# First-layer weight pieces split by one cast and one subtraction, and an expert's sums copied out one step earlier

## The chip, the cores and the metric

The kernel runs on one core of a Trainium2 chip. The metric is the device time of one execution in microseconds; the time quoted for a kernel is the median of several runs. The engines that matter here are TensorE (PE, matrix products; PEld is its weight load), VectorE (DVE), ScalarE (ACT), GpSimd (POOL) and SyncE (SP), whose queue issues nearly all DMAs. Each engine works through its own instructions in order, and the engines wait for one another by semaphores.

## The reference

Three layers follow one another. A recurrence over 768 positions for 4 x 8 heads gives 3072 tokens of width 320. Each token then goes to one of 8 experts (a two-layer network with ReLU), and the result goes through a dense two-layer network with a leaky ReLU:

```
x = attn_out.transpose(0, 2, 1, 3).reshape(3072, 320)
...
h = np.maximum(np.einsum('ecd,edf->ecf', disp, w1), 0.0)     # w1: 8 x 320 x 1024
y = np.einsum('ecf,efd->ecd', h, w2)                         # w2: 8 x 1024 x 320
out[i] = gate_w[i] * y[expert_idx[i], pos[i]]
...
h = x @ w_in                                                 # 320 x 2048
out = np.maximum(0.01 * h, h) @ w_out                        # 2048 x 320
```

## The kernel before

The recurrence fills the first 537 us of the profiled execution, the experts 537 to 810 us, the dense network the rest. The change touches the second and third of these, in the function `moe`.

**Split numbers.** Products are made in a rounded 32-bit format. So that nothing is lost, each operand is split in two: the rounded value (a cast, on ACT) and the rest (a subtraction on DVE). A first-layer weight matrix has 320 rows, 128 + 128 + 64. A piece `q` of it covers all 320 rows and 512 columns; it is loaded into one of two buffers `raw` of 128 x 1536, the last 64 rows into partitions 0 to 63 of the third part (L946, L947). `split(n)` makes the tile `wq` of it, six parts of 512 columns: for the 256 full rows by one cast (L961) and one subtraction (L964); for the 64 last rows by a cast for part 5 (L962), a cast to the other half of the partitions for part 4 (L963), a subtraction (L965), and a cast of that rest back into part 5 (L966), so that parts 5 and 4 hold in 128 partitions what their two products need. A piece `o` (second-layer weights, L972 to L975) has no such remainder.

**Steps.** An expert has eight blocks m = 0 to 7 of 128 hidden units. Step i of the loop makes in this order: `do_a(i)`, the eight first-layer products of block i into `ph` (L1000), then ReLU into `gh` on ACT (L1051) and the rest `gl` on DVE (L1052); on m = 0, 2, 4, 6 `split` of a piece that is needed an expert later (q, q, o, o) and the load of the piece after next; a part of a repacking of 64-bit weights, in 22 portions, that POOL and DVE share (`cv1`: POOL L1102 to L1104; `cv2`: DVE L1113 to L1116, then POOL L1117; `cv0` loads a portion, `cv3` writes one back, L1122); on m = 2, 4, 6 the transposes of the next expert's tokens (L1035 to L1041); and last `do_b(i-2)`, the eight second-layer products of the block two steps back, added up in the PSUM tiles y0, y1, y2 (L1065 to L1068). After the last block of an expert `do_b` copies the sums out: y0 on ACT (L1071), y1 on DVE (L1072), y2 on both (L1073, L1074). There is one buffer for each of y0, y1, y2, so the next expert's first second-layer products wait for these copies.

Below, *boundary k* (k = 1 to 7) is the place where PE turns from expert k-1's sums to expert k's. At step i = 8k+1 the copies of expert k-1 are issued; at step 8k+2 come the first products of expert k into y0.

**The first layer's product** of one block is eight matmuls: for each of the two full parts rounded x rounded, rounded x rest, rest x rounded (L996), and two for the 64 last rows (L998), where `xt` part 4 holds the rounded tokens in its lower half and their rest in its upper half.

Of the kernel before, what the change touches and what calls it, by code (L numbers as in the profile page):

```python
# [10 lines left out]
ALU = mybir.AluOpType  # L11
# [914 lines left out]
def moe(ctx, tc, I, out, R, eng, wi):  # L926

    nc = tc.nc
    V, A, P, T, S = eng
# [10 lines left out]
    def load(n):  # L940
        if n >= len(pieces):
            return
        kind, i = pieces[n]
        r = raws[n] = R.raws[n % 2]
        if kind == 'q':
            S.dma_start(r[:, 0:1024], I['wqa'][i] if i < 16 else wi[0][i - 16])  # L946
            S.dma_start(r[0:64, 1024:1536], I['wqb'][i] if i < 16 else wi[1][32 * (i - 16):32 * (i - 16) + 32].rearrange("p (r f) -> (p r) f", f=512))  # L947
        else:
            S.dma_start(r[:, 0:1280], I['wo'][i] if i < 16 else wi[2][i - 16])

    def split(n):
        if n >= len(pieces):
            return
        kind, i = pieces[n]
        r = raws.pop(n)
        if kind == 'q':
            t = kp.tile([128, 6, 512], F32R, tag="wq", name="wq", bufs=4)
            wqs[i] = t
            tf = t.bitcast(F32)
            r3 = r.rearrange("p (c f) -> p c f", c=3)  # L960
            A.copy(t[:, 0:2], r3[:, 0:2])  # L961
            A.copy(t[0:64, 5], r3[0:64, 2])  # L962
            A.copy(t[64:128, 4], r3[0:64, 2])  # L963
            V.tensor_tensor(t[:, 2:4], r3[:, 0:2], tf[:, 0:2], ALU.subtract)  # L964
            V.tensor_tensor(t[0:64, 4], r3[0:64, 2], tf[0:64, 5], ALU.subtract)  # L965
            A.copy(t[64:128, 5], tf[0:64, 4])  # L966
        else:
            t = kp.tile([128, 4, 640], F32R, tag="wo", name="wo", bufs=4)
            wos[i] = t
            tf = t.bitcast(F32)  # L970
            r3 = r[:, 0:1280].rearrange("p (k c) -> p k c", k=4)
            A.copy(t[:, :, 0:320], r3)  # L972
            if i < 16:
                V.tensor_tensor(t[:, :, 384:640], r3[:, :, 0:256], tf[:, :, 0:256], ALU.subtract)
                V.tensor_tensor(t[:, :, 320:384], r3[:, :, 256:320], tf[:, :, 256:320], ALU.subtract)  # L975
            else:
                V.tensor_tensor(t[:, :, 320:640], r3, tf[:, :, 0:320], ALU.subtract)
# [14 lines left out]
    def gemm_a(ph, n, xt, wq, mm):  # L992
        o = 128 * mm
        seq = []
        for c in range(2):
            seq += [(wq[:, c, o:o + 128], xt[:, c, 0:n]), (wq[:, c, o:o + 128], xt[:, 2 + c, 0:n]), (wq[:, 2 + c, o:o + 128], xt[:, c, 0:n])]  # L996

        seq += [(wq[:, 5, o:o + 128], xt[:, 4, 0:n]), (wq[:, 4, o:o + 128], xt[:, 4, 0:n])]  # L998
        for k, (l, r) in enumerate(seq):
            T.matmul(ph, l, r, start=k == 0, stop=k == 7)  # L1000

# [2 lines left out]
    def prep_g(g):  # L1004
        if g < NG:
            o, n = GRP[g]
            sl = slice(o, o + n)
            split_x(('g', g), n, [Y[:, 0, sl], Y[:, 1, sl]], Y[0:64, 2, sl])
            S.dma_start(gid[:, g, 0:n // 128], R.ctab[sl].rearrange("(b p) c -> p b c", p=128))


    with ExitStack() as c1:
# [3 lines left out]
        def load_x(e):  # L1016
            if e >= NE:
                return
            w = cx.tile([TW, 4, XC], F32, tag="win", name="win", bufs=2)
            wins[e] = w  # L1020
            R.after(S.dma_start(w, R.xs[e * REG:e * REG + WIN].rearrange("(k p) c -> p k c", p=TW)), R.puts)
# [23 lines left out]
        def do_a(i):  # L1045
            e, m = divmod(i, 8)
            ph = ps.tile([128, 512], F32, tag="h", name="ph", bufs=3)[:, 0:WIN]
            gemm_a(ph, WIN, xts[e], wqs[2 * e + m // 4], m % 4)
            gh = kp.tile([128, 512], F32R, tag="gh", name="gh", bufs=3)
            gl = kp.tile([128, 512], F32R, tag="gl", name="gl", bufs=3)  # L1050
            A.activation(gh[:, 0:WIN], ph, AF.Relu)  # L1051
            V.scalar_tensor_tensor(gl[:, 0:WIN], ph, 0.0, gh.bitcast(F32)[:, 0:WIN], ALU.max, ALU.subtract)  # L1052
            gs[i] = gh, gl

        def do_b(i):
            e, m = divmod(i, 8)
            if m == 0:
                ys[e] = [ps.tile([128, 512], F32, tag=f"y{c}", name=f"y{c}", bufs=1)[:, 0:WIN] for c in range(3)]
            y = ys[e]
            gh, gl = gs.pop(i)  # L1060
            gh, gl = gh[:, 0:WIN], gl[:, 0:WIN]
            wo = wos[2 * e + m // 4][:, m % 4]
            for c in range(3):
                hi = wo[:, 128 * c:128 * c + 128]
                T.matmul(y[c], hi, gh, start=m == 0, stop=False)  # L1065
                if c < 2:
                    T.matmul(y[c], wo[:, 384 + 128 * c:512 + 128 * c], gh, start=False, stop=False)
                T.matmul(y[c], hi, gl, start=False, stop=m == 7)  # L1068
            if m == 7:
                at = ds(R.base[e], WIN)  # L1070
                A.copy(Y[:, 0, at], y[0])  # L1071
                V.tensor_copy(Y[:, 1, at], y[1])  # L1072
                A.copy(Y[0:64, 2, at], y[2][64:128])  # L1073
                V.tensor_tensor(Y[0:64, 2, at], y[2][0:64], Y[0:64, 2, at], ALU.add)  # L1074
                R.after(S.dma_start(R.ctab[at], R.xs[e * REG:e * REG + WIN, D:D + 2]), R.puts)
# [15 lines left out]
        def cv0(k):  # L1091
            if 0 <= k < len(cv):
                cs[k] = cx.tile([128, 1024], I32, tag="cv", name="cv", bufs=2)
                S.dma_start(cs[k][:, 0:2 * cv[k][2]], cv[k][0].bitcast(I32))

        def cv1(k):
            if 0 <= k < len(cv):
                n = cv[k][2]
                hl = cs[k][:, 0:2 * n].rearrange("p (c two) -> p c two", two=2)
                h = hl[:, :, 1].bitcast(F32)  # L1100
                m = cx.tile([128, 512], F32, tag="cvm", name="cvm", bufs=2)[:, 0:n]
                P.tensor_tensor(m, h, h, ALU.mult)  # L1102
                P.tensor_scalar(m, m, THR * THR, None, ALU.is_ge)  # L1103
                P.tensor_tensor(m, m, h, ALU.mult)  # L1104
                cs[k] = hl, m

        def cv2(k):
            if 0 <= k < len(cv):
                n = cv[k][2]
                hl, m = cs.pop(k)  # L1110
                lo, a = hl[:, :, 0].bitcast(mybir.dt.uint32), hl[:, :, 1]
                g = cx.tile([128, 512], I32, tag="cvg", name="cvg", bufs=1)[:, 0:n]
                V.tensor_scalar(a, m.bitcast(I32), 0x07FFFFFF, 3, ALU.bitwise_and, ALU.logical_shift_left)  # L1113
                V.scalar_tensor_tensor(g, m.bitcast(I32), -0x40000000, a, ALU.bitwise_and, ALU.bitwise_or)
                V.tensor_scalar(a, g, -0x00800000, None, ALU.bitwise_and)
                V.scalar_tensor_tensor(m, lo, 2.0 ** -52, a.bitcast(F32), ALU.mult, ALU.mult)  # L1116
                P.tensor_tensor(m, m, g.bitcast(F32), ALU.add)  # L1117
                cs[k] = m

        def cv3(k):  # L1120
            if 0 <= k < len(cv):
                S.dma_start(cv[k][1], cs.pop(k))  # L1122
# [9 lines left out]
        load(4); load(5)  # L1132
        kc = 0
        for i in range(8 * NE + 2):
            if i < 8 * NE:
                e, m = divmod(i, 8)
                do_a(i)
                at = (0, 2, 4, 6) if e else (2, 3, 5, 6)
                if m in at:
                    n = 4 * (e + 1) + at.index(m)  # L1140
                    split(n)
                    load(n + 2)
                if i == 3:
                    R.places()
                if m == 5:
                    R.place(e)
                if m == 4:
                    load_x(e + 2)
                if i == 2:
                    cv0(0)  # L1150
                    cv0(1)
                elif i == 4:
                    cv1(0)
                elif i > 4 and m in (3, 5, 7):
                    cv3(kc - 1)
                    cv2(kc)
                    cv0(kc + 2)
                elif i > 4 and m in (0, 4, 6):
                    cv1(kc + 1)
                    kc += 1  # L1160
                if m in (2, 4, 6):
                    prep_x1(e + 1, (m - 2) // 2)
            if i >= 2:
                do_b(i - 2)
            if i == 8 * NE - 2:
                prep_g(0)
# [276 lines left out]
```

## Time and profile before

| | us |
|---|---|
| median of 3 runs (1154.49, 1155.58, 1165.28) | 1155.58 |
| the profiled execution | 1167.16 |
| its span, first to last instruction | 1165.4 |
| PE busy | 987.0 (85%) |
| DVE busy | 796.7 (68%) |
| ACT busy | 630.8 (54%) |
| POOL busy | 479.8 (41%) |
| mean granted TensorE clock | 0.922 |

Busy shares are averages over stages that differ: PE is busy 75% of the time in the first 537 us and 98% in the last 340. The granted clock is given as a share of full speed: 1.00 is 2.4 GHz and 0.50 is 1.2 GHz, and values between are means over a stretch in which both occur. In a timeline a row is one instruction, or several alike, with its start, its length, and in brackets the idle time of its engine just before it and what ended that. A recorded length of a DVE or POOL instruction can hold time in which it stood still after its start.

### The profile page before, as it was taken

To read this page: it belongs to the slowest core of one execution; us is meant where nothing else is said; L and a number is where in the kernel's file an instruction comes from. 1 tells how busy PE (TensorE), PEld (TensorE's weight loads), DVE (VectorE), ACT (ScalarE), POOL (GpSimd) and SP (SyncE) were. 2 spreads that over 40 slices of the span, in tenths; PEclk is the share of its full clock that TensorE was granted. 3 is DMA by queue.
4 is the path that set the end of the run, shared out by engine and by line. 5 is a ranking of instruction groups with operands and counts; after the bars stand their busy time and mean duration, and the time that the engine had idled before them with its cause. 6 is when DMAs were issued, how large, how long until landed. Compare 5 with 4: busy or idle time off the path is not lost.

```text
span 1165.4 us, 32129 instructions
## 1 busy us (share of the span) xinstructions
PE 987.0 (85%) x13099; PEld 874.8 (75%) x13099; DVE 796.7 (68%) x1877; ACT 630.8 (54%) x1486; POOL 479.8 (41%) x575
## 2 busy tenths in 40 slices
PE   4566777977777878995998888989999999999997
PEld 3455666766666667774887777878989999999997
DVE  8986878999999969434776667776664545343453
ACT  6144577867777688994544444444543434343343
POOL 7334336545556446201354435452639191000100
PEclk9766799979989889997998889999999999999999
DMA  7539465455554532423654455643201010000000
GB/s 207 191 80 258 125 184 149 134 121 135 152 114 125 145 81 56 115 54 109 217 170 143 150 164 155 183 138 112 93 22 57 15 44 6 18 12 12 23 13 14
DMA packets 132459, 125.19 MB, mean 107 GB/s; under 512 B 90448, under 2 KB 98256, under 8 KB 132304
## 3 DMA queue, kind: packets, MB, share of 16 engines
q1 hardware_dynamic: 130000, 115.17, 35.3%
q0 software_dynamic: 2304, 7.89, 1.9%
q8 instruction: 105, 1.72, 0.6%
q14 instruction: 50, 0.41, 0.1%
HBM read 98.86 MB, written 24.20 MB: 106 GB/s over the span
## 4 chain that ended last, share of the span: by engine, by line
PE 38%; DVE 16%; ACT 12%; issue 10%; POOL 5%; DMA 4%; SPq 1%; POOLq 0%; ACTq 0%; DVEq 0%
PE ph L1000 14%; PE py L641 4%; ACT Z L294 3%; PE oy L1204 3%; PE oy L1203 3%; PE oy L1202 3%; ACT NI L294 2%; DVE Tt L472 2%; DVE tmp L470 2%; DMA wc<-cvm 2%; ACT MV L294 1%; POOL cvm L1103 1%; PE tr L609 1%; PE y L1065 1%; PE ch L589 1%
## 5 line engine op out<-in xcount | busy, mean ns | idle before, releaser
L1000 PE MATMUL ph<-xt,wq 128*128 128x512 f32 (+2 forms) x1408 | 318.4, 370 | 1.9 <-DVE xt L1041 1.9
L1000 PEld LDWEIGHTS ph<-xt,wq 128*128 128x128 f32 x1408 | 254.4, 194 | 33.0 <-DVE xt L1041 2.7
L1182 DVE TENSOR_TENSOR gf<-gf,ph 128x512 f32<-128x512 f32 (+1 forms) x112 | 68.4, 611 | 102.3 <-ACT gf L1181 102.0
L1186 DVE TENSOR_TENSOR gl<-gf,gh 128x512 fp32r<-128x512 f32 (+1 forms) x112 | 76.0, 679 | 70.1 <-ACT gh L1185 70.1
L294 ACT COPY Z<-tr 40x512 f32<-40x512 f32 x192 | 101.0, 539 | 39.6 <-PE tr L609 36.9
L1181 ACT ACTIVATE gf<-ph 128x512 f32<-128x512 f32 (+1 forms) x112 | 60.0, 535 | 110.0 <-PE ph L1000 109.7
L1212 POOL DMA_INDIRECT out_dram<-ob,gid x24 | 23.9, 996 | 221.9 <-ACT ob L1211 216.7
L1185 ACT CAST gh<-gf 128x512 fp32r<-128x512 f32 (+1 forms) x112 | 62.6, 559 | 91.9 <-DVE gf L1182 91.9
L641 PE MATMUL py<-Z,RE 128*32 128x40 f32 x1536 | 78.8, 215 | 24.2 <-DVE RE L630 24.0
L1065 PE MATMUL y<-gh,wo 128*128 128x448 f32 x192 | 76.1, 397 | 22.5 <-ACT Y L1071 22.5
L641 PEld LDWEIGHTS py<-Z,RE 128*32 128x32 f32 x1536 | 68.9, 122 | 32.0 <-DVE RE L630 27.1
L1204 PE MATMUL oy<-wo,gl 128*128 128x320 f32 x288 | 89.2, 310 | 0.2 <-DVE gl L1186 0.2
L1202 PE MATMUL oy<-wo,gh 128*128 128x320 f32 x288 | 88.9, 309 | 0.0
L1203 PE MATMUL oy<-wo,gh 128*128 128x320 f32 x288 | 88.9, 309 | 0.0
L1051 ACT ACTIVATE gh<-ph 128x448 fp32r<-128x448 f32 x64 | 34.8, 544 | 91.0 <-PE ph L1000 90.7
L472 DVE TENSOR_TENSOR Tt<-Tt,tmp 128x30 f32<-128x30 f32 (+19 forms) x275 | 77.0, 311 | 0.6
L1068 PE MATMUL y<-gl,wo 128*128 128x448 f32 x192 | 73.7, 384 | 0.0
L609 PE MATMUL tr<-ident,MV 128*104 128x128 f32 x384 | 63.4, 298 | 9.5 <-DVE AE L422 4.9
L470 DVE TENSOR_TENSOR tmp<-Mu,Tt 128x30 f32<-128x30 f32 (+19 forms) x275 | 68.1, 277 | 0.7
L1117 POOL TENSOR_TENSOR cvm<-cvm,cvg 128x512 f32<-128x512 f32 (+1 forms) x22 | 26.2, 1191 | 94.9 <-DVE cvm L1116 94.9
L630 DVE TENSOR_TENSOR RE<-tr,maskP 64x128 f32<-64x128 f32 x144 | 41.4, 287 | 34.7 <-PE tr L622 17.8
L589 PE MATMUL ch<-MV,NI 128*40 128x40 f32 x1472 | 53.8, 221 | 13.1 <-issue 6.2
(185 smaller groups left out, 2340.6 us busy)
## 6 DMA issues: line engine op xcount, KB each, us to landing
KB<-in_kbT_dram SPq DMA_DIRECT2D x24, 512.0 KB, 5.3
RE<-in_rT_dram SPq DMA_DIRECT2D x48, 256.0 KB, 3.6
AE<-in_aT_dram SPq DMA_DIRECT2D x20, 512.0 KB, 5.3
raw<-in_wo_dram SPq DMA_DIRECT2D x16, 640.0 KB, 4.2
raw<-in_wqa_dram SPq DMA_DIRECT2D x16, 512.0 KB, 4.5
w<-in_wT_dram SPq DMA_DIRECT2D x24, 264.0 KB, 4.5
xs<-maskZ SPq DMA_DIRECT2D x8, 563.5 KB, 9.2
win<-xs SPq DMA_DIRECT2D x8, 563.5 KB, 6.7
```

Source lines behind the costliest of these rows:

```text
L294: (E.copy if E is A else E.tensor_copy)(o, i)
L470: op(e, d, lambda E, tv=tv, k=k, lo=lo, h=h, m=m: E.tensor_tensor(tv, Mu[:, k:k + 1, k + 1:].broadcast_to([128, h - lo, m]), Tt[:, lo:h, k ...
L472: op(e, d, lambda E, tv=tv, k=k, lo=lo, h=h: E.tensor_tensor(Tt[:, lo:h, k + 1:], Tt[:, lo:h, k + 1:], tv, ALU.subtract), [('tmp', x)], [t ...
L609: E.transpose(c['t'][0:104, q, :], MV[:, 4 * h + q], ident)
L641: E.matmul(py[32 * g:32 * g + 32, b, col:col + 40], RE[:, j, p, :], Z[:, p, ZC[j]:ZC[j] + 40], start=True, stop=True)
L1000: T.matmul(ph, l, r, start=k == 0, stop=k == 7)
L1065: T.matmul(y[c], hi, gh, start=m == 0, stop=False)
L1068: T.matmul(y[c], hi, gl, start=False, stop=m == 7)
L1186: V.tensor_tensor(gl, gf, gh.bitcast(F32), ALU.subtract)
L1202: T.matmul(o, gh[:, sl], w[:, 0:320], start=m == 0, stop=False)
L1203: T.matmul(o, gh[:, sl], w[:, 320:640], start=False, stop=False)
L1204: T.matmul(o, gl[:, sl], w[:, 0:320], start=False, stop=m == 15)
```

## The change

Four edits. The 64 last rows are loaded twice, into both halves of the partitions. The split of a q piece becomes one cast and one subtraction over all 1536 columns; the six parts of `wq` are now three rounded ones and three rests. The products take them from their new places, with the same eight matmuls. And at step 8k+1 `do_b` of the last block of expert k-1, with the copies, is put ahead of `do_a` and everything else in that step.

```
-            S.dma_start(r[0:64, 1024:1536], I['wqb'][i] if i < 16 else ...)
+            for o in (0, 64):
+                S.dma_start(r[o:o + 64, 1024:1536], I['wqb'][i] if i < 16 else ...)
...
-            A.copy(t[:, 0:2], r3[:, 0:2])
-            A.copy(t[0:64, 5], r3[0:64, 2])
-            A.copy(t[64:128, 4], r3[0:64, 2])
-            V.tensor_tensor(t[:, 2:4], r3[:, 0:2], tf[:, 0:2], ALU.subtract)
-            V.tensor_tensor(t[0:64, 4], r3[0:64, 2], tf[0:64, 5], ALU.subtract)
-            A.copy(t[64:128, 5], tf[0:64, 4])
+            A.copy(t[:, 0:3], r3)
+            V.tensor_tensor(t[:, 3:6], r3, tf[:, 0:3], ALU.subtract)
...
-            seq += [..., (wq[:, 2 + c, o:o + 128], xt[:, c, 0:n])]
+            seq += [..., (wq[:, 3 + c, o:o + 128], xt[:, c, 0:n])]
-        seq += [(wq[:, 5, o:o + 128], xt[:, 4, 0:n]), (wq[:, 4, o:o + 128], xt[:, 4, 0:n])]
+        seq += [(wq[:, 2, o:o + 128], xt[:, 4, 0:n]), (wq[:, 5, o:o + 128], xt[:, 4, 0:n])]
...
         for i in range(8 * NE + 2):
+            last = i >= 2 and (i - 2) % 8 == 7
+            if last:
+                do_b(i - 2)
             if i < 8 * NE:
                 e, m = divmod(i, 8)
                 do_a(i)
...
-            if i >= 2:
+            if i >= 2 and not last:
                 do_b(i - 2)
```

In the changed program the lines behind the split stand three lower in number: the cast is L962 (ACT), the subtraction L963 (DVE), the doubled load L948, the first-layer products L997, the copies of the sums L1068 to L1071, the repacking's first DVE line L1110, its write-back L1119.

DVE at boundary 2, before: from the `gl` of expert 2's block 0 over the split of that step (m = 0) and the copies of expert 1's sums to the first row of the split at m = 2 (`Y` is the tile that takes the sums).

```order
L1052 SCALAR_TENSOR_TENSOR gl_9958<-ph_9948,gh_9957 128x448
L964 TENSOR_TENSOR wq_9961<-raw0_76,wq_9961 128x1024
L965 TENSOR_TENSOR wq_9961<-raw0_76,wq_9961 64x512
L1052 SCALAR_TENSOR_TENSOR gl_9991<-ph_9981,gh_9990 128x448
L1072 ISA
L1072 COPY Y_9357<-y1_9765 128x448
L1074 ISA
L1074 TENSOR_TENSOR Y_9357<-y2_9766,Y_9357 64x448
L1052 SCALAR_TENSOR_TENSOR gl_10017<-ph_10007,gh_10016 128x448
L964 TENSOR_TENSOR wq_10020<-raw1_77,wq_10020 128x1024
```

The same place in the changed program:

```order
L1049 SCALAR_TENSOR_TENSOR gl_9942<-ph_9932,gh_9941 128x448
L963 TENSOR_TENSOR wq_9945<-raw0_76,wq_9945 128x1536
L1069 ISA
L1069 COPY Y_9357<-y1_9747 128x448
L1071 ISA
L1071 TENSOR_TENSOR Y_9357<-y2_9748,Y_9357 64x448
L1049 SCALAR_TENSOR_TENSOR gl_9984<-ph_9974,gh_9983 128x448
L1049 SCALAR_TENSOR_TENSOR gl_9997<-ph_9987,gh_9996 128x448
L963 TENSOR_TENSOR wq_10000<-raw1_77,wq_10000 128x1536
```

The two subtractions are one, and the copies of y1 and y2 stand right behind it; the `gl` of the next block has moved behind them.

ACT at the same place, before: the split of the step m = 0, the next `gh`, and the copies of expert 1's sums.

```order
L961 CAST wq_9961<-raw0_76 128x1024
L962 CAST wq_9961<-raw0_76 64x512
L963 CAST wq_9961<-raw0_76 64x512
L966 CAST wq_9961<-wq_9961 64x512
L1051 ACTIVATE gh_9990<-ph_9981 128x448
L1071 ISA
L1071 COPY Y_9357<-y0_9764 128x448
L1073 ISA
L1073 COPY Y_9357<-y2_9766 64x448
```

And in the changed program:

```order
L962 CAST wq_9945<-raw0_76 128x1536
L1068 ISA
L1068 COPY Y_9357<-y0_9746 128x448
L1070 ISA
L1070 COPY Y_9357<-y2_9748 64x448
L1048 ACTIVATE gh_9983<-ph_9974 128x448
```

Four casts, the last of which took its input from DVE, are one that takes it from the load alone; the copies stand right behind it and ahead of the next `gh`.

SP's queue in the middle of expert 1, before: the loads of a q piece, the next expert's tokens (`win`), and the write-back of a repacked portion (`wb`).

```order
L946 DMA raw0_76<-in_wqa_dram 128x1024
L947 DMA raw0_76<-in_wqb_dram 64x512
L1021 DMA win_9824<-xs_60 112x4x322
L918 TENSOR_LOAD bi_75
L1122 DMA wb_81<-cvm_9697 128x512
```

And in the changed program:

```order
L946 DMA raw0_76<-in_wqa_dram 128x1024
L948 DMA raw0_76<-in_wqb_dram 64x512 x2
L1018 DMA win_9807<-xs_60 112x4x322
L918 TENSOR_LOAD bi_75
L1119 DMA wb_81<-cvm_9683 128x512
```

One more load of 128 KB stands ahead of the write-back. On PE the eight products of expert k-1's last block come ahead of the first-layer products of step 8k+1 instead of behind them; their number and sizes are the same.

## Rows read from the trace of the kernel before

**Rows 1.** Waits between 537 and 810 us: who for whom, total us, times, longest.

```profile
ACT wq L966 <- DVE wq L965: 47.1, 17, 7.2
DVE cv L1113 <- POOL cvm L1104: 28.5, 12, 4.9
...
PE y L1065 <- ACT Y L1071: 22.5, 7, 4.7
```

**Rows 2.** Stretches (length, PE, PEld, DVE, ACT, POOL busy, clock, DMA share, GB/s).

```profile
587.05:594.52 7.47, 4.98 (x18) 4.28 (x17) 4.82 (x7) 5.79 (x10) 3.36 (x3) 0.77 0.37 94
594.52:618.41 23.89, 23.89 (x125) 22.00 (x123) 17.87 (x26) 8.58 (x14) 12.55 (x10) 1.00 0.61 185
618.41:628.18 9.77, 5.88 (x18) 5.13 (x17) 6.99 (x9) 5.88 (x10) 4.90 (x3) 0.65 0.38 106
...
685.94:696.48 10.54, 5.84 (x19) 5.09 (x18) 7.77 (x10) 5.87 (x10) 4.51 (x4) 0.68 0.46 123
...
754.19:759.14 4.95, 3.68 (x19) 3.03 (x18) 3.71 (x6) 4.47 (x8) 2.36 (x2) 1.00 0.46 133
784.20:792.27 8.07, 5.22 (x18) 4.37 (x17) 5.34 (x7) 5.34 (x9) 3.89 (x3) 0.79 0.33 90
```

**Rows 3.** Timeline of PE around boundary 2.

```profile
609.91 1.78 PE L1000 MATMUL ph<-xt,wq 128*128 128x448 f32 x8
...
613.15 1.78 PE L1000 MATMUL ph<-xt,wq 128*128 128x448 f32 x8
...
618.01 0.55 PE L1035 MATMUL pt<-ident,win 112*128 112x112 f32 x4
622.45 0.74 PE L1065 MATMUL y<-gh,wo 128*128 128x448 f32 x1 [3.89 <-ACT Y L1071]
...
628.18 0.36 PE L1065 MATMUL y<-gh,wo 128*128 128x448 f32 x1
```

**Rows 4.** Timeline of ACT around boundary 2.

```profile
613.75 0.62 ACT L963 CAST wq<-raw 64x512 fp32r<-64x512 f32 x1
620.78 0.62 ACT L966 CAST wq<-wq 64x512 fp32r<-64x512 f32 x1 [6.41 <-DVE wq L965]
...
621.87 0.53 ACT L1071 COPY Y<-y 128x448 f32 x1
```

**Rows 5.** Timeline of DVE around boundary 2.

```profile
614.50 0.43 DVE L1113 TENSOR_SCALAR cv<-cvm 128x512 int32<-128x512 int32 x1 [3.60 <-POOL cvm L1104]
...
616.77 0.62 DVE L1052 SCALAR_TENSOR_TENSOR gl<-ph,gh 128x448 fp32r<-128x448 f32 x1
617.30 2.01 DVE L964 TENSOR_TENSOR wq<-raw,wq 128x1024 fp32r<-128x1024 f32 x1
619.23 1.52 DVE L965 TENSOR_TENSOR wq<-raw,wq 64x512 fp32r<-64x512 f32 x1
...
622.54 0.62 DVE L1072 COPY Y<-y 128x448 f32 x1
...
624.49 1.23 DVE L964 TENSOR_TENSOR wq<-raw,wq 128x1024 fp32r<-128x1024 f32 x1 [0.28 <-ACT wq L961]
625.63 0.68 DVE L965 TENSOR_TENSOR wq<-raw,wq 64x512 fp32r<-64x512 f32 x1
```

**Rows 6.** Timeline of POOL around boundary 2.

```profile
616.93 1.30 POOL L1117 TENSOR_TENSOR cvm<-cvm,cvg 128x512 f32<-128x512 f32 x1 [2.46 <-DVE cvm L1116]
618.18 2.02 POOL L1102 TENSOR_TENSOR cvm<-cv 128x512 f32<-128x512 f32 x1
```

**Rows 7.** Chain that ended last, from boundary 2 to 3 (start, us, what).

```profile
637.44 6.57 DMA wc<-cvm
...
648.12 0.44 DVE cv L1113
```

**Rows 8.** A stretch of the same columns as above, behind the loads.

```profile
641.50:644.00 2.50, 2.50 (x14) 2.31 (x14) 1.71 (x4) 0.55 (x1) 0.00 (x0) 1.00 1.02 345
```

**Rows 9.** DMA issues by line: times, KB each, median us to landing.

```profile
raw<-in_wqb_dram SPq DMA_DIRECT2D x16, 128.0 KB, 4.6
```

More of the change, by code (lines that the diff above doesn't have):

```diff
@@ L946, in load @@
             S.dma_start(r[:, 0:1024], I['wqa'][i] if i < 16 else wi[0][i - 16])
-            S.dma_start(r[0:64, 1024:1536], I['wqb'][i] if i < 16 else wi[1][32 * (i - 16):32 * (i - 16) + 32].rearrange("p (r f) -> (p r) f", f=512))
+            for o in (0, 64):
+                S.dma_start(r[o:o + 64, 1024:1536], I['wqb'][i] if i < 16 else wi[1][32 * (i - 16):32 * (i - 16) + 32].rearrange("p (r f) -> (p r) f", f=512))
         else:
@@ L995, in gemm_a @@
         for c in range(2):
-            seq += [(wq[:, c, o:o + 128], xt[:, c, 0:n]), (wq[:, c, o:o + 128], xt[:, 2 + c, 0:n]), (wq[:, 2 + c, o:o + 128], xt[:, c, 0:n])]
-        seq += [(wq[:, 5, o:o + 128], xt[:, 4, 0:n]), (wq[:, 4, o:o + 128], xt[:, 4, 0:n])]
+            seq += [(wq[:, c, o:o + 128], xt[:, c, 0:n]), (wq[:, c, o:o + 128], xt[:, 2 + c, 0:n]), (wq[:, 3 + c, o:o + 128], xt[:, c, 0:n])]
+        seq += [(wq[:, 2, o:o + 128], xt[:, 4, 0:n]), (wq[:, 5, o:o + 128], xt[:, 4, 0:n])]
         for k, (l, r) in enumerate(seq):
```

## The prediction

> **What bounds the kernel now.** I read the waits of the expert phase first, then PE's stretches there, then the timelines of the engines around one place where PE stands still. In the waits two rows belong together: PE waits 22.5 us in 7 pieces for ACT's copy of y0, and ACT waits 47.1 us in 17 pieces for DVE's L965, inside the split that the change rewrites [rows 1]. The seven pieces are the seven boundaries. Between them PE is full: 23.89 us busy of 23.89 at clock 1.00 [rows 2]. At a boundary the work is one `do_b` and one `do_a`, 3.24 us at full clock (613.15 - 609.91) [rows 3]. It takes instead 7.47 us at boundary 1, 9.77 at boundary 2 (boundaries 3 and 5 are like it), 10.54 at 4, 4.95 at 6 and 8.07 at 7 [rows 2]. So the losses are 4.2, three times 6.5, 7.3, 1.7 and 4.8, together 37.5 us. They have two parts: PE stands (at 2: 9.77 - 5.88 = 3.89 us), and its busy time is 5.88 instead of 3.24, because after the stand the granted clock is for a while at its lower level, 1.2 GHz (0.65 is the mean of the stretch). At boundary 6, after 1.27 us of standing, the clock stays at 1.00 [rows 2].
>
> Why PE stands, at boundary 2. Call T = 614.50 the start of DVE's repacking L1113, which had waited 3.60 us for POOL. `gl` follows at T+2.3, then L964 and L965 to 620.75 (T+6.25) [rows 5]. ACT had its three casts done at 614.4 and now waits 6.41 us to do L966; behind it in the queue stand a `gh` and the copy of y0, which starts at 621.87, and PE goes on at 622.45 = T+7.95 [rows 3, 4]. PE itself was free at 618.56 = T+4.06.
>
> T itself hangs on the boundary before it: from the first second-layer matmul after boundary 2 (628.18) to the next T (648.12) it is 19.94 us [rows 3, 7], a chain over an ACT cast, a DVE subtraction, SP's loads, the write-back that lands 6.57 us after its issue, and POOL. PE needs 23.89 us for its work from there to the next boundary. So experts run as a loop: what the boundary takes, plus the longer of these two ways.
>
> **The change part by part.**
>
> *ACT's wait goes.* L962 to L966 and their wait fall away. One cast over the same columns reads only the load and is not longer than the three that are done at 614.4 today. The copy of y0 then starts as soon as PE has summed it. Since `do_b` of the last block comes before the second `do_a`, PE has it done at 614.8 (609.91 plus three halves of 1.62 us). So y0 is free long before PE wants it at T+4.06. What is late next is y1, copied by DVE behind the subtraction.
>
> *DVE's subtraction.* Undisturbed, the two were 1.23 and 0.68 us long; at the boundary 2.01 and 1.52 [rows 5]. The rows tell why: L964 starts at 617.30, POOL's L1117 runs to 618.23, and L964 ends 1.08 us after that; L1102 ends 0.89 us after L964's end; L965 ends 0.55 us after L1102's [rows 5, 6]. They take turns, each whole. One wide subtraction starts with the same wait, then needs 1.08 + 0.55 (1.23 - 0.68, for the further 512 columns) = 1.63 us: it ends at 619.86, without a second turn to wait for. The bounds: 1.8 us with no wait at all (ends 619.1), 3.45 us as the two together today (620.75). I take 619.86, since the row of L964 is the same instruction against the same neighbour. The Trainium skill, "SBUF — State Buffer", section "Who interferes with whom", says that a VectorE instruction with two inputs in SBUF and a GpSimd instruction that reads SBUF lock each other out whole, whoever comes first; by that rule, too, the wide one waits once.
>
> *The copy of y1* (0.62 us [rows 5]) stands right behind and ends at 620.45 = T+5.95; `gl` of the next block, with its wait for `gh`, now comes later and is wanted only by the `do_b` after next. PE does y0's three matmuls at T+4.06 to T+4.7, stands until T+5.95, then has five matmuls and a `do_a`: 5/8 of 1.62 + 1.62 = 2.65 us. The next second-layer matmul starts at T+8.6 at full clock, where it was T+13.68.
>
> *The added load.* 20 loads of 128 KB. In five of the loops such a load stands ahead of the write-back on which POOL waits. Behind the loads the DMA engines are full, share 1.02 at 345 GB/s [rows 8]; at some 300 GB/s, 128 KB is 0.45 us. Below, it could be nothing, if the queue has room; above, a landing of its own, 4.6 us [rows 9]. I take 0.45, since the full engines, not a latency, set that stretch. The Trainium skill speaks against the form chosen here: in "SBUF — State Buffer", section "Can I just issue two DMAs to hit both halves?", two transfers into the two halves of the partitions go one after the other, and its table gives 196 GB/s for partitions 0 to 63. By these an estimate of the load's price is 0.67 us and the sum would be 1.1 us worse; no run here shows it yet.
>
> *The loop then.* From T to the next T: 8.6 + 19.94 + 0.45 = 29.0 us, against 33.62 today (648.12 - 614.50). PE's work in it is 23.89 + 3.24 = 27.13, so PE still stands 1.9 us at boundaries 2 to 5. Does the clock fall then? Standing 1.27 us it did not, 2.49 us (boundary 1, clock 0.77) it did [rows 2]. 1.9 lies between, and is broken by three matmuls. I take the fall, somewhat likelier than not, at what it cost at boundary 1: 4.98 - 3.24 = 1.74, say 1.8 us. That leaves 3.7 us lost.
>
> *The sum.* Boundary 1 stood 2.49 us; y1 is 2.0 us earlier (T+5.95 for T+7.95) and the three matmuls fill 0.6, so nothing is left: 4.2. Boundaries 2, 3, 5: 6.5 - 3.7 = 2.8 each, 8.4. Boundary 4: 7.3 - 3.7 = 3.6. Boundary 6: 1.27 us less than 2.0: 1.7. Boundary 7 stood 8.07 - 5.22 = 2.85; 2.0 and 0.6 off leave 0.25, with the added load 0.8: 4.0. Together 21.9 us.
>
> *Worth nothing:* the splits ahead of the first expert (PE waits there for tokens) and the two q splits in the dense phase, where PE, not ACT, sets the pace (98% busy). Of each piece ACT is freed of at least two casts of 0.62 us [rows 4], 25 us over 20 pieces, which lie under PE's work and would count only if ACT were the bound. The eight matmuls are the same.
>
> The profiled execution took 1167.16 us, 11.6 above the median; the boundaries are worked out in it, and I carry the difference over: 1155.6 - 21.9 = 1133.7, say **1134 us**.
>
> **The rivals.**
>
> *The clock holds* at 1.9 us of standing: 4 x 1.8 = 7.2 us more, 1126.5. For it: boundary 6. Against it: boundary 1.
>
> *Prices at their upper ends:* the subtraction takes 3.45 us, y1 comes at T+6.85 and about 0.9 us is added at five boundaries, with the added load 1 us instead of 0.45 in five loops, and clock falls at 1 and 7 too (3.6): 10.9 us less gain, 1145.
>
> *The gain is given back in the loop:* the added load costs its whole landing, 4.6 us, before the write-back: 4.15 us more in five loops, 20.8 of 21.9: 1155, no change. For it: the write-back waits behind the loads in one queue; against it: the full engines in rows 8.
>
> *Slower:* the added load and the write-back go strictly one after the other, so that each of six loops (that before boundary 7 too) pays a landing like the write-back's, 6.57 us [rows 7]: 6 x 6.1 = 36.7 less 21.9, so 1170. It decides from about (21.9 + 11.6)/6 = 5.6 us over my price per loop. Against it: the write-back shares full engines with 1.2 MB of loads ahead of it and still lands in 6.57 us.
>
> *The change doesn't do what it says:* y0 free early but T or y1 later by as much, because DVE, not ACT, was the limit. DVE has 6.99 of 9.77 us busy at boundary 2 [rows 2]; PE then stands as before and only 6 and 7 gain: about 1150.
>
> **How the numbers follow.** Forecast 0.46, clock holds 0.26, upper prices 0.16, given back in the loop or not done by DVE 0.08, slower 0.04. A measurement here can tell about 1% (11.6 us) from no change. Faster by more: the first two, and 0.10 of the third, where not all its prices are at their ends, 0.82. Within 1%: the other 0.06 and the 0.08, 0.14. Slower: 0.04. The range goes down to 1124 (the clock holds and the load costs nothing: 1126.5 - 5 x 0.45) and up to 1149 (all upper prices, on a kernel that measures 4 us above the median); the cases of no change and slower, 0.12, and some more at the lower end lie outside.
>
> **What would show it.** ACT's wait on DVE in the split is gone; PE's wait names DVE's copy of y1 instead of ACT's of y0, and is near 1.9 us at boundaries 2 to 5 and nearly none at 1, 6, 7; the wide subtraction is near 2.5 us at a boundary and 1.8 elsewhere; the distance from T to T is near 29 (31 with the clock's fall); the clock in the stretches is 1.00 at 1, 6 and 7. Wrong: a write-back that lands over 8 us after its issue, a subtraction over 3 us, or T-to-T distances near 33.

## The result and the profile after

The changed kernel takes 1133.23 us (median of 4: 1129.84, 1132.88, 1133.58, 1139.52) where the kernel before, measured beside it, takes 1158.80 (median of 4). The two medians lie 25.6 us apart; the measured ratio is 0.976, with a 95% interval of 0.972 to 0.979, which is some 28 us. The forecast was 1134, with a gain of 21.9 us from 1155.6.

| profiled execution, us | before | after |
|---|---|---|
| the execution | 1167.16 | 1129.84 |
| its span | 1165.4 | 1128.1 |
| ahead of the first tokens' transposes | 547.7 | 542.2 |
| expert stage: from there to the last second-layer product | 262.4 | 231.3 |
| dense stage | 355.3 | 354.6 |
| mean granted clock | 0.922 | 0.937 |

The profiled execution of the kernel before was slower than all four of its timed runs, and that of the changed kernel was the fastest of its four, so what lies between these two profiles is more than the gain between medians. Of the 37.3 us between the two spans, 31.1 lie in the expert stage and 0.7 in the dense one. The other 5.5 lie ahead of the first transposes, where the change alters only the first loads and splits of weights; I count them as spread between executions, since among the kernels below the same length goes from 539.2 us (e4) to 549.1 (e3).

The two rows that follow are the expert stage as a stretch, with the columns of [rows 2], first of the kernel before:

```profile
547.70:810.10 262.40, 237.36 (x1120) 214.44 (x1121) 186.70 (x269) 118.39 (x188) 119.39 (x88) 0.92 0.54 165
```

and of the changed kernel, with its stretches at boundary 2 and 4. These two begin earlier in PE's work than those in [rows 2], with the first-layer products of the block before the stand, and so hold 30 matmuls instead of 18; their lengths can't be set beside each other, their clocks can:

```profile
542.20:773.50 231.30, 223.41 (x1121) 202.78 (x1122) 178.96 (x253) 97.81 (x140) 122.05 (x88) 0.98 0.65 197
...
606.78:613.85 7.07, 5.53 (x30) 4.78 (x28) 7.04 (x9) 2.89 (x4) 6.06 (x4) 1.00 0.44 129
...
664.70:672.80 8.10, 5.59 (x30) 4.82 (x30) 8.03 (x10) 2.88 (x4) 4.97 (x4) 1.00 0.47 146
```

PE does the same products (1120 and 1121 records) in 223.41 us instead of 237.36, because the clock is 0.98 instead of 0.92; that is 13.95 of the 31.1 us. The rest, 17.2, is standing (25.04 us before, 7.89 after). At boundaries 2 and 4 the clock is 1.00, where it was 0.65 and 0.68.

The waits of the changed kernel between 530 and 790 us (who for whom, total, times, longest), beside [rows 1]:

```profile
ACT gh L1048 <- PE ph L997: 120.4, 62, 4.4
POOL cvm L1114 <- DVE cvm L1113: 57.0, 22, 5.8
DVE cv L1110 <- POOL cvm L1101: 28.1, 17, 5.0
...
PE y L1062 <- DVE Y L1069: 5.5, 3, 2.5
PE ph L997 <- DVE xt L1038: 1.6, 2, 1.4
```

ACT's 47.1 us for DVE inside the split are gone; what ACT now waits for in this stage is almost all products (120.4 us). PE's 22.5 us for ACT's copy of y0 are gone too. In their place stand 5.5 us in three pieces for DVE's copy of y1, at boundaries 2, 3 and 4 (1.54, 1.46 and 2.51 us).

DVE at boundary 2 of the changed kernel, as a timeline; T, the start of the repacking on DVE as in the prediction, is 605.19:

```profile
605.19 0.43 DVE L1110 TENSOR_SCALAR cv<-cvm 128x512 int32<-128x512 int32 x1 [3.41 <-POOL cvm L1101]
...
607.46 0.62 DVE L1049 SCALAR_TENSOR_TENSOR gl<-ph,gh 128x448 fp32r<-128x448 f32 x1
607.99 2.53 DVE L963 TENSOR_TENSOR wq<-raw,wq 128x1536 fp32r<-128x1536 f32 x1
610.44 0.61 DVE L1069 COPY Y<-y 128x448 f32 x1
...
612.57 1.74 DVE L963 TENSOR_TENSOR wq<-raw,wq 128x1536 fp32r<-128x1536 f32 x1
```

POOL at the same place:

```profile
607.62 1.29 POOL L1114 TENSOR_TENSOR cvm<-cvm,cvg 128x512 f32<-128x512 f32 x1 [2.46 <-DVE cvm L1113]
608.87 2.56 POOL L1099 TENSOR_TENSOR cvm<-cv 128x512 f32<-128x512 f32 x1
```

And PE, as a timeline too:

```profile
608.72 0.45 PE L1062 MATMUL y<-gh,wo 128*128 128x448 f32 x1
...
611.11 0.47 PE L1062 MATMUL y<-gh,wo 128*128 128x448 f32 x1 [1.54 <-DVE Y L1069]
...
613.85 0.36 PE L1062 MATMUL y<-gh,wo 128*128 128x448 f32 x1
```

Read DVE and POOL together. The subtraction starts at 607.99 while POOL's L1114 runs to 608.91, and ends at 610.52, which is 1.61 us after that. POOL's next instruction, L1099, is recorded from 608.87 and ends at 611.43, 0.91 us after the subtraction. Elsewhere the subtraction takes 1.74 us. PE has done y0's three products from 608.72 (T+3.53), stands, goes on with y1 at T+5.92 and makes the next block's products; the next second-layer product starts at T+8.66.

### The profile page after: what moved, and what is told of

It is laid out like the page before. It is cut to its first block, busy times and chain, and to the rows that moved or that the text cites. A ratio compares the mean times of both kernels' runs of the same rounds, so it can differ in the third digit from the quotient of the medians.

```text
span 1128.1 us, 32070 instructions
## 1 busy us (share of the span) xinstructions
PE 973.5 (86%) x13099; PEld 863.8 (77%) x13099; DVE 791.4 (70%) x1857; ACT 605.1 (54%) x1426; POOL 484.1 (43%) x575
## 3 DMA queue, kind: packets, MB, share of 16 engines
q0 software_dynamic: 2304, 7.89, 1.9%
## 4 chain that ended last, share of the span: by engine, by line
PE 40%; DVE 19%; issue 9%; ACT 9%; DMA 4%; POOL 3%; SPq 1%; DVEq 0%; POOLq 0%; ACTq 0%
PE ph L997 16%; PE py L641 3%; PE oy L1204 3%; PE oy L1203 3%; PE oy L1202 3%; ACT Z L294 2%; DVE Tt L472 2%; DVE tmp L470 2%; DVE AE L377 2%; DMA wc<-cvm 2%; ACT NI L294 2%; ACT MV L294 2%; DVE RE L630 1%; DMA wa<-cvm 1%; PE tr L609 1%
## 5 line engine op out<-in xcount | busy, mean ns | idle before, releaser
L997 PE MATMUL ph<-xt,wq 128*128 128x512 f32 (+2 forms) x1408 | 311.8, 365 | 1.7 <-DVE xt L1038 1.6
L997 PEld LDWEIGHTS ph<-xt,wq 128*128 128x128 f32 x1408 | 248.5, 190 | 31.8 <-DVE xt L1038 2.8
L1048 ACT ACTIVATE gh<-ph 128x448 fp32r<-128x448 f32 x64 | 34.9, 545 | 120.4 <-PE ph L997 120.4
L1062 PE MATMUL y<-gh,wo 128*128 128x448 f32 x192 | 72.6, 378 | 5.6 <-DVE Y L1069 5.5
L1065 PE MATMUL y<-gl,wo 128*128 128x448 f32 x192 | 70.4, 366 | 0.0
L431 POOL TENSOR_TENSOR AE<-AE,maskP 32x256 f32<-32x256 f32 x40 | 32.0, 805 | 72.4 <-ACT AE L294 68.6
```

## The experiments

The theory: the gain is the time that PE stood at the boundaries, and the lower clock behind it, set free because ACT's copies no longer queue behind a cast that waits for DVE; what is left is set by DVE's copy of y1. The rivals: the move of the copies does the work and the split little; the added load eats part of the gain in the loop over the write-back; or the clock alone tells the kernels apart. Each time is the median of its runs; each ratio is to the kernel before, run on the same chip, with its interval.

| run | time, us | ratio | expert stage of its profile |
|---|---|---|---|
| changed kernel | 1133.23 | 0.976 (0.972 to 0.979) | 231.3 |
| e8, the same again | 1135.68 | 0.978 (0.972 to 0.983) | 238.3 |
| e1, split alone | 1143.55 | 0.984 (0.981 to 0.987) | 237.8 |
| e2, move alone | 1154.94 | 0.993 (0.990 to 0.995) | 251.2 |
| e3, one load | 1134.49 | 0.974 (0.970 to 0.977) | 229.1 |
| e12, a load more, to a spare tile | 1140.98 | 0.981 (0.979 to 0.984) | 231.8 |
| e7, a load more, to the same place | 1164.99 | 1.002 (0.999 to 1.005) | 256.5 |
| e10, both halves by one transfer | 1186.07 | 1.020 (1.017 to 1.024) | 276.3 |
| e4, split one step later | 1134.53 | 0.976 (0.973 to 0.979) | 234.8 |
| e5, y1 copied three times | 1146.55 | 0.988 (0.981 to 0.994) | 244.3 |
| e6, copies of y0 and y1 exchanged | 1146.24 | 0.986 (0.980 to 0.993) | 244.8 |
| e9, write-back ahead of the loads | 1130.29 | 0.972 (0.970 to 0.975) | 228.3 |
| e11, e9 again | 1129.35 | a single run | 227.1 |

**The two parts apart.** e1 takes the changed kernel without the move:

```
         for i in range(8 * NE + 2):
-            last = i >= 2 and (i - 2) % 8 == 7
-            if last:
-                do_b(i - 2)
...
-            if i >= 2 and not last:
+            if i >= 2:
                 do_b(i - 2)
```

> Only the split and its double load are changed; the copies stay where they were before. The measure is the expert stage, from the first transposes of tokens to the first product of the dense network: 262.4 us before, 231.3 with the change. If the split carries the gain (ACT no longer waits for DVE), DVE makes the next gl ahead of the copy of y1, so that copy comes about 0.55 us later: stands of about 2.1, 2.0 and 3.1 us at boundaries 2 to 4 and some tenths elsewhere, stage 233 to 236 us, or up to 7 us more if the clock falls. If the moved copies carry it: stage 250 us or more, and 1150 us or more in all.

e2 takes the kernel before with the move alone, the same lines the other way round.

> Only the last block's products and the copies are moved ahead; the split is the old one. By the theory that ACT's wait for DVE inside the split sets the boundary, the copy of y0 now stands right behind L966, which still waits until T+6.25: y0 is free at about T+7.5 instead of T+7.95, half a microsecond for each of seven boundaries, stage 257 to 260 us. If the moved copies carry the gain: stage below 245 us.

PE's wait for the sums in e1 (total, times, longest):

```profile
PE y L1062 <- DVE Y L1069: 9.2, 6, 2.9
```

DVE's timeline at boundary 2 in e1:

```profile
611.14 2.54 DVE L963 TENSOR_TENSOR wq<-raw,wq 128x1536 fp32r<-128x1536 f32 x1
613.60 0.61 DVE L1049 SCALAR_TENSOR_TENSOR gl<-ph,gh 128x448 fp32r<-128x448 f32 x1
614.13 0.61 DVE L1069 COPY Y<-y 128x448 f32 x1
```

The same wait in e2:

```profile
PE y L1065 <- ACT Y L1071: 17.6, 6, 4.6
```

The expert stage of e2 as a stretch:

```profile
545.60:796.80 251.20, 228.95 (x1121) 206.98 (x1122) 188.09 (x269) 118.09 (x188) 120.90 (x88) 0.96 0.55 172
```

ACT's timeline at boundary 2 in e2:

```profile
618.53 0.62 ACT L966 CAST wq<-wq 64x512 fp32r<-64x512 f32 x1 [6.56 <-DVE wq L965]
619.17 0.54 ACT L1071 COPY Y<-y 128x448 f32 x1
```

The split alone gives 0.0164 of 1164.3, 19 us; the move alone 0.0072, 8 us; both together 28 and, run again, 26. So the first rival falls. With the split, one `gl` stands between the subtraction and y1's copy (613.60), and the copy starts at T+5.79 instead of T+5.25: the move takes that instruction away, 0.54 us. Without the split, the move leaves ACT's 6.56 us as they were; the copy of y0 merely has one `gh` less ahead of it. PE stands 4.9 us less for the sums than in [rows 1] (2.3 of which come back as waits for the next tokens, 4.2 instead of 1.9 us), and its busy time is 228.95 instead of 237.36 because the clock fell at three boundaries of e2 instead of six. My 257 to 260 us for its expert stage reckoned with less standing, and not with fewer falls: a miss of 6 to 9 us. Whether the move or the execution lies behind the fewer falls, one profile can't tell; the 8 us rest on the timed runs. How much the move adds on top of the split is told by the times only roughly: the interval of e1 lies above that of the changed kernel and overlaps that of e8, and one profile can't tell it (237.8 us beside 231.3 and 238.3).

**The added load.** e3 loads the last rows once; the upper half of the partitions holds zeros, so part of what the two products of the last rows add up is left out.

```
-            for o in (0, 64):
+            for o in (0,):
                 S.dma_start(r[o:o + 64, 1024:1536], ...)
...
+        for r in R.raws:
+            V.memset(r[64:128, 1024:1536], 0.0)
```

> The changed kernel without the second load of the 64 last rows; the upper half of that part is filled with zeros once, so the results of half of two products per block are left out. By my price (0.45 us per loop, which counts only where PE stands, boundaries 2 to 4): stage 229.5 to 231 us. If the load paid a landing of its own, 4.6 us, the stands would vanish: stage 226 us.

e7 loads the upper half twice:

```
-            for o in (0, 64):
+            for o in (0, 64, 64):
```

> The changed kernel with the upper half of the 64 last rows loaded twice, a third load of 128 KB per piece. By my price a further 0.45 us in each loop that has a stand: stage 232 to 234 us. If a load paid a landing of its own (4.6 us) the stage would grow by 15 us or more, past 246.

e12 makes the third load into a tile that nobody reads:

```
+            s = kp.tile([128, 512], F32, tag="scr", name="scr", bufs=1)
+            S.dma_start(s[64:128], ...)
```

> The changed kernel with a third load of 128 KB per piece that goes to a tile of its own which nobody reads, so that it waits for no earlier transfer as the third load of the same place did. By my price, 0.45 us per loop: T to T near 29.5 us, stage 232 to 240 us with the changed kernel's spread, 1134 to 1142 us. If a load as such, without a wait on SP, pays a landing: 1155 us or more, as the third load to the same place.

e10 makes one transfer of the two, with a source that repeats itself:

```
-            for o in (0, 64):
-                S.dma_start(r[o:o + 64, 1024:1536], ...)
+            b = ...
+            S.dma_start(r[:, 1024:1536], b.unsqueeze(0).broadcast_to([2, 64, 512]))
```

> The changed kernel with the two loads of the 64 last rows made one transfer to all 128 partitions, its source read twice. The bytes stay the same. If the bytes are the price, stage as in the changed kernel (231 to 238 us). If it is the second transfer (its issue, or its use of half the partitions), as without the second load: 229 to 232 us.

e3 and the changed kernel can't be told apart (0.974 and 0.976). e12 is some 5 us slower (0.981 beside 0.976 and 0.978), with intervals that overlap. What the load costs shows in the chain of the changed kernel that ended last, from boundary 2 to 3 (start, us, what):

```profile
621.51 0.49 SPq L948
622.04 0.59 SPq L948
622.68 0.59 SPq L1018
...
623.72 6.33 DMA wc<-cvm
```

The second L948 is the added load: about 0.6 us to issue it, ahead of the write-back. The write-back lands in 6.33 us, not later than the 6.57 of [rows 7]. In e7 a third load, to a place that is being loaded already, costs the whole gain. By my expectation that would have meant that every load pays a landing, but the waits of SP's queue show another reason:

```profile
SPq L948 <- DMA raw<-in_wqb_dram: 59.2, 14, 7.1
...
SPq L948 <- DMA raw<-wb: 17.9, 4, 5.6
```

A load to the place of a load still under way waits, by a semaphore, for that one's landing, and everything behind it in SP's queue waits too: 77.1 us in 18 pieces, where the changed kernel has none of L948 for an earlier load. So e7 does not measure what a load costs the DMA engines. In e12 the waits of this kind are few (the spare tile's load is L950 there):

```profile
SPq L950 <- DMA scr<-in_wqb_dram: 2.6, 2, 1.6
```

and there the load is cheap. e10 came out far from both of its expected values (276.3 us for 231 to 238 or 229 to 232). In e10 ACT's cast waited for the one transfer; a row of the waits:

```profile
ACT wq L962 <- DMA raw<-in_wqb_dram: 36.4, 13, 6.0
```

The chain of e10 that ended last went, ahead of T at boundary 2 (626.01), over a write-back of 10.66 us (start, us, what):

```profile
611.24 10.66 DMA wb<-cvm
```

Stretches of e10 behind its loads (columns as in [rows 2]):

```profile
619.00:621.00 2.00, 2.00 (x7) 1.80 (x6) 0.00 (x0) 1.86 (x2) 0.00 (x0) 0.50 0.55 210
...
625.00:627.00 2.00, 2.00 (x12) 1.85 (x11) 0.96 (x2) 0.55 (x1) 0.97 (x1) 1.00 0.13 49
```

As the other transfers end, a DMA share of 0.13 at 49 GB/s is left. 0.13 of 16 engines is 2, and the outer dimension of this source is 2. This is what the Trainium skill says in "DMA: Bandwidth & Descriptors", section "Why a DMA increments its semaphore by 16 and not by 1": the number of engines is the largest, up to 16, that divides the slowest dimension of both patterns. The trace agrees, in this one share; no run here has a source with another outer dimension. The two loads of the change, with 64 rows each, are the better form: 0.976 of the kernel before, against 1.020.

**The order on DVE and ACT.** e4 puts the split of the steps m = 0 one step later, e5 makes the copy of y1 three times, e6 exchanges which engine copies y0 and y1. Their edits in this order:

```
-                at = (0, 2, 4, 6) if e else (2, 3, 5, 6)
+                at = (1, 2, 4, 6) if e else (2, 3, 5, 6)
```

> The changed kernel with the split of step m = 0 moved to m = 1, behind the copies of the sums. If the wide subtraction ahead of the copy of y1 is all that is left of the stand, y1 is free at T+3.5, PE does not stand at any boundary, and the stage falls from 231.3 to about 226 us (5.5 us of stands). If the loop over the write-back and POOL limits the stage anyway, the stand moves elsewhere and the stage stays at 230 to 232 us.

```
-                V.tensor_copy(Y[:, 1, at], y[1])
+                for _ in range(3):
+                    V.tensor_copy(Y[:, 1, at], y[1])
```

> The changed kernel with DVE's copy of y1 made three times, 2 x 0.54 us more between the subtraction and the copy of y2; the first of them does not free y1, the last does. By the theory that this copy ends the stand, stands grow by 1.1 us at boundaries 2 to 4 (to 2.6, 2.5 and 3.6) and small ones appear at 1, 5, 7: stage 231.3 plus 4 to 7 us if the clock holds. If stands over about 2.5 us lower the clock, three to four falls of 1.8 us come on top: 241 to 245 us. If DVE's copy is not what PE waits for: no change.

```
-                A.copy(Y[:, 0, at], y[0])
-                V.tensor_copy(Y[:, 1, at], y[1])
+                V.tensor_copy(Y[:, 0, at], y[0])
+                A.copy(Y[:, 1, at], y[1])
```

> The changed kernel with the engines of two copies exchanged: DVE copies y0, ACT copies y1. Now PE's first product waits for the copy behind the subtraction, and the stand is not shortened by three matmuls: 0.6 us more at boundaries 2 to 4 (2.2, 2.1, 3.1 us) and up to 0.5 at 1, 5 and 7. Stage 233 to 235 us if the clock holds as in the changed kernel, 237 to 242 if stands of this length lower it, as one of 2.49 us did before.

PE's wait between the experts' products in e4:

```profile
PE ph L997 <- DVE xt L1038: 9.6, 6, 3.2
```

The same in e5:

```profile
PE y L1062 <- DVE Y L1070: 13.2, 7, 3.0
...
PE ph L997 <- DVE xt L1038: 3.3, 2, 3.0
```

And in e6:

```profile
PE y L1062 <- DVE Y L1068: 8.3, 4, 3.5
PE ph L997 <- DVE xt L1038: 3.6, 2, 3.4
PE y L1062 <- ACT xt L1034: 2.0, 1, 2.0
```

In e5 two copies more, about 1.1 us, turn three waits for y1 into seven, 5.5 into 13.2 us, and the kernel is 11 to 13 us slower (its interval lies above that of the changed kernel and overlaps that of e8): y1's copy on DVE is what ends last. In e6 it is y0, wanted three products earlier, that stands behind the subtraction, and the kernel is about as much slower (one of its four executions stood apart at 4056.06 us, the others took 1144.3 to 1146.7; I can't explain the one); its stage of 244.8 us lies above the 237 to 242 expected, as the clock fell at four places. In e4 y1's copy comes at T+2.8, the wait for it is gone as thought, and the time does not move: PE now waits 9.6 us in six pieces for the rest of the next tokens (L1038), DVE's work, and the stage takes 234.8 us, against 230 to 232 expected for this case. Ahead of one of these waits (2.96 us, until 660.22) DVE's timeline in e4 shows the same wait for POOL as at T:

```profile
653.53 0.43 DVE L1110 TENSOR_SCALAR cv<-cvm 128x512 int32<-128x512 int32 x1 [3.40 <-POOL cvm L1101]
...
659.55 0.62 DVE L1038 TENSOR_TENSOR xt<-pt,xt 64x448 fp32r<-64x448 f32 x1
```

So taking away the last wait at a boundary is not worth its length. I read it so that the loop over the write-back, through POOL and DVE, hands the wait to the next place; the next run tests that.

**The loop.** If so, what shortens the loop should help where e4 did not. e9 puts the loads of the steps m = 2, 4 and 6 and of the tokens behind the write-back of the following step in SP's queue:

```
+        late = []
...
-                    load(n + 2)
+                    if e and m in (2, 4, 6):
+                        late.append(n + 2)
+                    else:
+                        load(n + 2)
...
-                if m == 4:
+                if m == 4 and not e:
                     load_x(e + 2)
...
                     cv3(kc - 1)
+                    while late:
+                        load(late.pop())
+                    if m == 5 and e:
+                        load_x(e + 2)
```

> The changed kernel with the loads of steps m = 2, 4, 6 and of the next expert's tokens put behind the write-back of the step that follows. If the loop over the write-back sets when T comes, the write-back of m = 5 lands without 1.3 MB of loads ahead of it, some 2 to 3 us earlier; T comes earlier by as much, the stands at boundaries 2 to 4 (1.5, 1.5, 2.5 us) vanish, and with them the falls of the clock: stage 224 to 227 us in every execution. If T is set by something else (POOL's own work, DVE's queue), stands and stage stay as in the changed kernel, 231 to 238 us.

e11 is the same kernel again.

> The kernel with the write-back first once more, for its spread: stage 224 to 227 us again, and no granted clock below 1.00 at a boundary, if its stands are gone; a spread as wide as the changed kernel's (7 us) if not.

SP's queue in e9, as a timeline ahead of boundary 3:

```profile
622.42 0.33 SPq L1119 DMA_DIRECT2D wc<-cvm  x1
624.29 0.33 SPq L946 DMA_DIRECT2D raw<-in_wqa_dram  x1
624.67 1.13 SPq L948 DMA_DIRECT2D raw<-in_wqb_dram  x2
```

PE's waits in e9:

```profile
PE ph L997 <- DVE xt L1038: 4.3, 2, 3.8
```

The expert stage of e9 as a stretch:

```profile
543.30:771.60 228.30, 223.36 (x1121) 203.62 (x1122) 182.37 (x253) 97.78 (x140) 133.29 (x89) 0.98 0.67 200
```

No wait for a sum is left at any boundary; T to T is 27.7 us on average over six loops ((745.05 - 579.03)/6), where the changed kernel has 28.5 and, run again, 29.5, and PE alone needs 27.13 by the prediction's sum. Its stage stands 4.9 us in all (228.30 - 223.36). One fall of the clock is left in each of its two profiles, ahead of T at boundary 1 and next to a wait for the tokens (3.85 us in e9, 2.69 in e11); so the expected stage of 224 to 227 us without a fall was missed, by 1.3 us in e9 and 0.1 in e11. The kernel takes 1130.29 us, the fastest of all, and 1129.35 in e11. Its interval overlaps those of the changed kernel, so that it beats the kernel before is shown, and that it beats the changed one by some 4 us is likely and not shown.

**The same kernel again.**

> The changed kernel itself again, for its spread: stage 231 us within 2 us if the clock holds every time; 233 to 240 us, with a granted clock below 1.00 at boundary 4, if its stand of 2.5 us is at the edge.

Three stretches of e8: the 5 us behind two of its waits (2.50 and 2.41 us long), and the expert stage:

```profile
643.15:648.15 5.00, 5.00 (x17) 4.49 (x18) 3.74 (x5) 0.49 (x1) 4.20 (x3) 0.66 0.64 140
674.56:679.56 5.00, 5.00 (x17) 4.53 (x18) 3.81 (x6) 0.55 (x1) 1.55 (x2) 0.68 0.64 140
543.30:781.60 238.30, 227.18 (x1120) 205.47 (x1121) 178.26 (x253) 97.76 (x140) 122.98 (x88) 0.97 0.64 191
```

And the 5 us behind the 2.51 us of boundary 4 in the first profile of the changed kernel:

```profile
670.03:675.03 5.00, 5.00 (x25) 4.65 (x26) 4.96 (x8) 0.55 (x1) 1.56 (x2) 1.00 0.66 140
```

PE does 17 matmuls in 5 us at clock 0.66, and 25 at 1.00. Waits of the same length end in the lower clock in one execution and not in the other. By the clock alone, e8's two falls cost 227.18 - 223.41 = 3.8 us, some 1.9 each; PE also stands 3.2 us more (11.1 for 7.9). That is the 7 us between the two profiles of one kernel.

The longer stand ahead of the first of the falls comes from the loop before it. The chain of e8 that ended last, ahead of boundary 3 (start, us, what):

```profile
624.70 8.44 DMA wc<-cvm
633.20 1.05 POOL cvm L1099
```

The write-back that landed in 6.33 us in the first profile lands here in 8.44. The loop from boundary 2 to 3 is 31.1 us instead of 29.0, PE stands 2.50 us instead of 1.46, and then the clock falls; with the fall, the next loop is 31.4 instead of 29.9. Behind it the write-back took 5.46 us (6.16 in the first profile), so the late one is an event of that execution. That the longer stand brought the fall is likely, and not shown: in the first profile one of 2.51 us did not.

## Why the prediction was right, step by step

**ACT's wait and what is late next: right.** The 47.1 us are gone, and PE's wait names DVE's copy of y1. ACT's busy time falls by 25.7 us (630.8 to 605.1; 25 worked out) without showing anywhere else.

**The subtraction: right.** Forecast: the same wait for POOL's turn, then 1.63 us. Measured: 1.61 us after POOL's end, 2.53 in all; six of the seven at boundaries took 2.53 or 2.54. Two instructions had taken 2.01 and 1.52 [rows 5], because each waited for a turn of its own. The rule of "SBUF — State Buffer", "Who interferes with whom" in the Trainium skill, on which the prediction leaned in a sentence beside it, agrees with POOL's L1099 too: recorded from 608.87, it ends only after the subtraction. y1's copy starts at T+5.25 (forecast T+5.33), the next second-layer product at T+8.66 (T+8.6).

**The loop: right.** From that product to the next T it is 20.3 us at boundary 2 (634.17 - 613.85), where 19.94 + 0.45 were put down; T to T is 29.0, 29.0, 29.9 and 27.8 us from boundary 1 to 5, where 29.0 was forecast, and in e8 31.4 in the loop that begins with the fall at boundary 3, where 31 was (the one that begins with the fall at boundary 4 took 30.1). A write-back over 8 us, which I had named as what would prove the forecast wrong, occurred once, in e8 (8.44 us): it lengthened one loop by 2 us and did not become the rule. At boundary 5 the way back was shorter, 19.1 us (691.90 - 672.76), and PE does not stand there at all, against my 1.9.

**The added load: the price near, its reason wrong.** I took 0.45 us, from full DMA engines. The chain shows about 0.6 us of SP's issuing, and a write-back that lands no later than before (and in the same loop of e3, without the added load, 5.87 us after its issue: half a microsecond sooner, from one execution). The rival that a landing is added is refuted by e3 and e12. By the prediction's estimate from the table in "SBUF — State Buffer" of the Trainium skill the price would have been 0.67 us; that is near the 0.6, but what the chain shows is issue, not transfer, so it says nothing for or against that table. e7 shows the form in which the rival of "no change" would have come true: a load that must wait in SP's queue.

**The clock: the term that was mis-sized.** I took the fall at boundaries 2 to 5, 4 x 1.8 = 7.2 us. In the first profile it came at none, in the second at two. So the gain was 31.1 and 24.1 us in the two expert stages, where my sum has 29.1 with no fall and 25.5 with two; the 28 and 26 us by the timed ratios lie between my sum with four falls (21.9) and with none. The 2.0 us by which the first profile beats the sum with none are about the size of a second miss: PE stood 5.5 us at boundaries 2 to 5, and not 4 x 1.9 = 7.6. What I had set up as two rivals, the clock falls and the clock holds, are cases of one kernel in different executions. I had treated as a property of the kernel what differs from one execution to the next, also because the write-back, and with it the stand, does (6.33 and 8.44 us in the same loop). That the 1134 I gave lies so close to 1133.23 is partly luck: the gain was put too low by 4 to 6 us, and the time of the kernel before, 1155.58 instead of the 1158.80 of the comparison, by 3.2 us, and the two errors offset each other.

**Nothing in the dense stage: right.** 355.3 and 354.6 us.

**The two parts: only partly foreseen.** The prediction gave no price to the move by itself. It is worth 8 us alone and 7 to 9 behind the split by the medians (0.984 against 0.976 and 0.978), of which the rows explain 0.54 us per boundary directly. The remainder would be fewer falls of the clock and shorter loops; this was argued, and not measured by itself.

## What to carry to other kernels

When engines lock each other out by turns, one wide instruction waits for one turn; and a cast that waits for another engine's result should not stand in a queue ahead of the copies that free an accumulator. Behind the wait that ends last there is often a loop (here load, repacking, write-back): if removing the wait moves nothing, as in e4, shorten the loop, as in e9. Where waits of one length are followed by the lower clock in one execution and not in another, forecast both cases for each wait, not one for the kernel.

## What the runs showed of the hardware

The length of PE's stand does not decide by itself whether the clock falls. Between 560 and 812 us of the 14 profiles (e7 and e10 among them), no stand up to 1.83 us was followed by the lower clock within 5 us, other than those with a longer stand right behind; of the 44 from 1.89 to 3.60 us, 28 were (in e7 and e10 several lie within 5 us of another stand); of the 8 from 3.67 us on, all. What sets the middle ones apart isn't settled here.

A second load to a place whose first load is still under way held the whole issuing queue, in which the program waits for the first one's landing, for up to 7.1 us each time (e7), whereas the same bytes to another tile cost some 5 us in the whole kernel, if anything (e12). And a single transfer over 128 partitions was far slower than two over 64 each (ratios 1.020 and 0.976); with its source's outer dimension of 2 it kept about 2 of 16 DMA engines busy (share 0.13).
